# Seven early head pairs instead of six, query maxima as rows of one small product, key-value sums turned through DRAM

## The chip, the cores and the metric

The kernel runs on one core of one Trainium2 chip. The metric is the device time of one execution in microseconds (us), the median of three runs. The core's five instruction queues run side by side and meet at semaphores: TensorE (PE, with PEld for its weight loads), VectorE (DVE), ScalarE (ACT), GpSimd (POOL) and SyncE (SP), which here issues every DMA. Each queue runs its instructions in the order in which they were written.

## The reference

Linear attention over 8 batches, 8 heads, 576 tokens and head size 64, followed by a feed-forward block over all 4608 tokens:

```python
def phi(x):
    proj = np.einsum('bhsd,df->bhsf', x, w_phi)            # 64 -> 128 features
    proj = proj - np.max(np.abs(proj), axis=-1, keepdims=True)
    return np.concatenate([np.exp(proj), np.exp(-proj)], axis=-1)
q_p, k_p = phi(q), phi(k)
kv = np.einsum('bhsf,bhsd->bhfd', k_p, v)
z = np.sum(k_p, axis=2)
num = np.einsum('bhsf,bhfd->bhsd', q_p, kv)
den = np.einsum('bhsf,bhf->bhs', q_p, z)[..., None] + 1e-06
attn = num / den
# then, with x = attn as 4608 x 512:
g = np.maximum(x @ w_in, 0.0) ** 2                         # 512 -> 2048
out = g @ w_out                                            # 2048 -> 512
```

So each token's query projection loses its own largest absolute value over the 128 features before the two exponentials.

## The kernel before, in words

**Work units.** Two heads make a pair; there are 32 pairs, four to a batch. Each pair's result (576 tokens x 128 columns, transposed) goes into a ring buffer in SBUF as two float16 parts (`ring`, lines L733 and L736). The feed-forward block takes the tokens in 18 chunks of 256, each chunk in 8 slices of 256 hidden columns. A slice is one `gemm1` (24 matmuls, L912), three elementwise steps on ACT and DVE (L921 to L930, and the subtraction at L266), and one `gemm2` (12 matmuls, L940). A chunk needs all four pairs of its batch: chunks 0 and 1 lie in batch 0 (pairs 0 to 3), chunk 2 needs pairs 4 to 7 too.

**Early pairs.** The first `EARLY` = 6 pairs run in a form of their own (function `early`), while the feed-forward weights are still being prepared and POOL is not yet free for reductions. A pair's steps are: key projection on PE (`k_main` L490, `k_tail` L496) with maxima, subtraction and exponentials; key-value sums on PE (`kv_main` L546, `kv_tail` L551) and the sums over tokens (L578); then three copies that turn the 128 x 384 result around: ACT copies it from PSUM (`kvs`, L585), PE transposes three blocks (L590), ACT copies them back (`kz`, L593). The query is projected twice. First with tokens on the partitions (L605, tail L611), only so that DVE can take each token's maximum (`qm`, L616 and L620); then, per half of 288 tokens, with features on the partitions (L634). The second projection has the maximum of its own column subtracted by further matmuls into the same PSUM bank: the maxima stand as columns of `qm`, spread over 128 columns, times a negated identity `nident` (L643, six matmuls per half). Exponentials (L650, L652), numerators (L660) and denominators (L678) follow. The denominators go out and back through DRAM: `den<-sx` (L686), `rd<-rc` (L699), `rb<-rd` (L706, two DMAs). A product with the numerators (L714) gives the values that are written to the ring.

For the first `BANKS` = 4 pairs the first projections use PSUM banks that the feed-forward block needs later (`po`, `ph`). Later pairs use the single `pp` buffer, which all second projections use too, so there one user must have been read out before the next one may start.

**Late pairs.** Pairs 6 to 31 run in another form (`visit` and `late`): the key sums are turned by a DVE transpose (L797), one DMA to DRAM (`td`, L798) and eight DMAs back (`kz<-td`, L803), and the query maxima are taken by POOL (`partition_all_reduce`, L846).

**Weights.** Each of the 16 weight blocks is loaded raw (L381, L384; 1024 KB each) and passes through four or five steps on ACT (L401, L390, L422, L426, L435), two or three on DVE (L393, L397, L428) and one or two on POOL (L404, L266).

**What sets the order.** Every step is an `Op` with an engine, a written-down duration, a rank and a landing time for DMAs. `Plan.order` is a list scheduler that runs once on the host; it starts what is ready in the order of rank and writes the instructions of all queues in that order. Ranks are `PER_PAIR` = 4.5 per pair; weight blocks start at rank `PREP0` = 18; feed-forward slices at `LEAD` = 36.

```python
o = P.add("PE", 2.0, q_proj, [q_load[p], minus] + most, [("q", p), pq, ("qm", p)], R(x), mode=(ROWS, WHOLE))
kz = P.add("ACT", act_us(384), lambda: A.activation(
    out=kz_[p], in_=pv_["t", p][:, 0:384], func=AF.Copy), [o], [("pv", ("t", p)), ("kz", p)], R(3.1))
ld = P.add("SP", 2.7, load, [] if of_in else [raw_read[f]], [], rank - 3.0 + 0.3 * n, land=2.0)
```

## Time and profile before

| | |
|---|---|
| median of 3 runs (lowest, highest) | 1113.24 us (1112.3, 1113.45) |
| the profiled execution's own time | 1108.32 us |
| its span, first to last instruction | 1106.5 us |
| mean granted TensorE clock | 0.984 |
| busy: PE, DVE, ACT, POOL | 97%, 67%, 57%, 17% of the span |
| first `gemm1` | at 112.37 us |

The profile is one execution. Its own time is 1.8 us more than its span, and 4.9 us under the median of the runs. In the tables of stretches the columns after the stretch are its length and then, for PE, PEld, DVE, ACT and POOL, the busy time with the number of instructions, and at the end the granted clock (1.00 is full), the DMA share and GB/s. In a timeline a row is start, duration, engine, line, operation, output and inputs, count, and in square brackets the idle time before it with what ended that.

### The profile page before, as it was taken

The numbers are of one execution on the slowest core, as the hardware profiler recorded it, in microseconds if no ns is written. First come the engines' busy times: TensorE is split into PE (matmuls) and PEld (weight loads), VectorE is DVE, ScalarE is ACT, GpSimd is POOL, SyncE is SP. The second block draws the span as 40 slices with busy tenths as digits, with TensorE's granted clock in tenths as the row PEclk, the third lists the DMA queues.
The fourth block names the chain that finished last, engine by engine and source line by source line (L and its number), as shares of the span: only waits on it lengthen the run. The fifth ranks groups of instructions, "written<-read, shape, count | busy, mean of one in ns | idle before, by whom it ended". The sixth has DMA issues, their size and how long they took to land.

```text
span 1106.5 us, 19979 instructions
## 1 busy us (share of the span) xinstructions
PE 1071.9 (97%) x7882; PEld 831.4 (75%) x7882; DVE 739.1 (67%) x1538; ACT 633.5 (57%) x1125; POOL 183.9 (17%) x86
## 2 busy tenths in 40 slices
PE   7868999989999999999999999999999999999998
PEld 5645777767777777777777787777777777888886
DVE  6385988887787888787877687667786875121111
ACT  6787766555656666566665566655554655333332
POOL 1165533111102112111201111110111111000000
PEclk9987999999999999999999999999999999999999
DMA  9733312122122222121221111212111110000000
GB/s 336 266 104 121 104 56 73 55 74 55 55 73 55 73 55 74 55 74 54 74 53 62 36 52 55 74 55 73 43 48 30 36 32 30 11 20 20 1 20 20
DMA packets 68289, 73.50 MB, mean 66 GB/s; under 512 B 36836, under 2 KB 41828, under 8 KB 68196
## 3 DMA queue, kind: packets, MB, share of 16 engines
q1 hardware_dynamic: 68196, 72.23, 21.4%
q8 instruction: 62, 1.02, 0.4%
q14 instruction: 31, 0.25, 0.1%
HBM read 59.18 MB, written 12.99 MB: 65 GB/s over the span
## 4 chain that ended last, share of the span: by engine, by line
PE 74%; DVE 9%; ACT 3%; DMA 3%; issue 2%; POOL 1%; SPq 0%; DVEq 0%; POOLq 0%; ACTq 0%
PE po L940 31%; PE ph L912 29%; PE pv L546 3%; PE pp L833 2%; PE pn L764 2%; PE pp L490 2%; PE pv L764 2%; DMA rb<-rd 1%; PE pv L551 1%; DVE gl L266 1%; DVE pt L860 1%; PE pn L496 1%; DVE qe L266 1%; POOL mx L846 1%; DVE yt L864 1%
## 5 line engine op out<-in xcount | busy, mean ns | idle before, releaser
L912 PE MATMUL ph<-ring,win 128*128 128x256 f16 x3456 | 401.1, 273 | 0.3 <-DVE ring L736 0.3
L912 PEld LDWEIGHTS <-win 128*128 128x128 f16 x3456 | 328.4, 98 | 69.7 <-issue 32.8
L940 PE MATMUL po<-wout,gh 128*128 128x512 f32 x1152 | 371.2, 403 | 0.0
L940 PEld LDWEIGHTS po<-wout,gh 128*128 128x128 f32 x1152 | 207.1, 189 | 47.7 <-issue 5.3
L940 PE MATMUL po<-wout,gl 128*128 128x512 f32 x576 | 227.1, 394 | 3.5 <-DVE gl L266 3.5
L921 ACT ACTIVATE r<-ph,cw 128x512 f32<-128x512 f32 x144 | 98.6, 685 | 223.8 <-PE ph L912 223.4
L846 POOL PARTITION_ALL_REDUCE mx<-pt x52 | 113.8, 2188 | 638.9 <-ACT pt L840 602.6
L266 DVE TENSOR_TENSOR gl<-ph,gh 128x512 fp32r<-128x512 f32 x144 | 98.5, 684 | 158.4 <-ACT ph L930 156.4
L940 PEld LDWEIGHTS po<-wout,gl 128*128 128x128 f32 x576 | 108.6, 189 | 29.1 <-DVE gl L266 4.0
L923 ACT ACTIVATE gh<-r 128x512 fp32r<-128x512 f32 x144 | 90.9, 632 | 4.6
L930 ACT ACTIVATE ph<-r 128x512 f32<-128x512 f32 x128 | 74.7, 583 | 0.0
L786 ACT ACTIVATE n<-pn 128x320 f32<-128x320 f32 x26 | 11.4, 437 | 93.6 <-PE pn L764 93.6
L546 PE MATMUL pv<-e,v 128*64 128x256 f32 x512 | 62.8, 389 | 1.4 <-ACT kz L593 1.4
L266 DVE TENSOR_TENSOR qe<-pt,mx 128x576 f32<-128x576 f32 x52 | 39.3, 755 | 23.0 <-POOL mx L846 22.7
L860 DVE SCALAR_TENSOR_TENSOR pt<-qe,zc,pt 128x576 f32<-128x576 f32 x52 | 42.2, 812 | 12.8 <-ACT pt L858 11.9
L546 PEld LDWEIGHTS pv<-e,v 128*64 128x64 f32 x512 | 36.6, 141 | 18.0 <-issue 2.5
L851 ACT ACTIVATE qe<-qe 128x576 f32<-128x576 f32 x52 | 35.2, 676 | 24.8 <-DVE qe L266 24.6
L512 ACT ACTIVATE e<-e 128x512 f32<-128x512 f32 x64 | 39.7, 621 | 16.1 <-DVE e L509 16.1
L797 DVE STREAM_TRANSPOSE kvs<-pv 128x256 f32<-128x256 f32 x26 | 11.6, 445 | 54.1 <-PE pv L764 48.4
L858 ACT ACTIVATE pt<-qe,zc 128x576 f32<-128x576 f32 x52 | 39.9, 772 | 3.8
L537 DVE TENSOR_TENSOR es<-es,et 64x256 f32<-64x256 f32 x52 | 35.4, 681 | 9.8 <-ACT et L524 8.3
L864 DVE STREAM_TRANSPOSE yt<-pt 128x576 f32<-128x576 f32 x52 | 40.4, 778 | 1.5
(196 smaller groups left out, 1306.4 us busy)
## 6 DMA issues: line engine op xcount, KB each, us to landing
v<-in_vp_dram SPq DMA_DIRECT2D x32, 320.0 KB
k<-in_kp_dram SPq DMA_DIRECT2D x32, 288.0 KB
q<-in_qp_dram SPq DMA_DIRECT2D x32, 288.0 KB
rb<-rd SPq DMA_DIRECT2D x64, 144.0 KB
out_dram<-o SPq DMA_DIRECT2D x36, 256.0 KB
td<-kvs SPq DMA_DIRECT2D x26, 128.0 KB
kz<-td SPq DMA_DIRECT2D x208, 16.0 KB
raw0i<-in_w_in_dram SPq DMA_DIRECT2D x1, 1024.0 KB
```

The costliest lines, as they stand in the source:

```text
L266: eng.tensor_tensor(out=out_, in0=a, in1=b_, op=ALU.subtract)
L546: PE.matmul(out=to[64 * h:64 * h + 64, 0:256], lhsT=v_[p][:, t, h, :], rhs=e_[2 * p + h][:, t].rearrange("p s f -> p (s f)"), start=t == 0 ...
L764: PE.matmul(out=to[64 * h:64 * h + 64, :], lhsT=kz_[n][:, 128 * s_ + 64 * h:128 * s_ + 64 * h + 64], rhs=qe_[2 * n + h].rearrange("p (s x) ...
L846: o = P.add("POOL", par_us(S), lambda n=n, h=h: G.partition_all_reduce(mx_[n], pt_[p][:, h, :], channels=128, reduce_op=bass_isa.ReduceOp. ...
L858: o = P.add("ACT", act_us(S, 1), lambda h=h, qe=qe, y=y: A.activation(out=y(), in_=qe(0), func=AF.Copy, scale=zc_[p][:, 2 * h:2 * h + 1]), ...
L860: o = P.add("DVE", dve_us(S), lambda h=h, qe=qe, y=y: V.scalar_tensor_tensor(out=y(), in0=qe(1), scalar=zc_[p][:, 2 * h + 1:2 * h + 2], in ...
L864: o = P.add("DVE", dve_us(S), lambda n=n, y=y: V.transpose(yt_["y", n - 2 * EARLY], y()), [o], [("pt", p), ("yt", ("y", n - 2 * EARLY))], ...
L912: PE.matmul(out=ph[:, j, :], lhsT=win[w][:, t, 128 * ff:128 * ff + 128], rhs=ring[half][x][:, t, c0:c0 + T], start=k == 0, stop=k == 3 * K ...
L921: o = P.add("ACT", act_us(512, 1), lambda: A.activation(out=r_[n], in_=ph_[bank], func=AF.Relu, scale=cw[:, f, 0:1]), [g1], [("ph", bank), ...
L923: sq = P.add("ACT", act_us(512), lambda: A.activation(out=gh_[n], in_=r_[n], func=AF.Square), [o], [("r", n), ("gh", n)], Q)
L930: o = P.add("ACT", act_us(512), lambda: A.activation(out=ph_[bank], in_=r_[n], func=AF.Square), [sq], [("ph", bank), ("r", n)], Q)
L940: PE.matmul(out=po_[po[i][1]], lhsT=g[n][:, j, 128 * i:128 * i + 128], rhs=wout[f][w][:, j, :], start=(ff == 0 and s == 0), stop=(ff == 2 ...
```

## The change

- `EARLY` goes from 6 to 7 and `BANKS` from 4 to 5. One pair more takes the early form, and five pairs instead of four have their first projections in the feed-forward block's PSUM banks and their last product on POOL.
- The query maxima become rows. DVE transposes the 128 x 32 tile `qm` into `qt`; one DMA writes it to DRAM (`tq`); four DMAs read it back into row 0 and row 64 of a tile `pt` that is otherwise zero. Per half and head one matmul of 64 rows and 288 columns with a stationary operand of -1 subtracts them (`minus`, `row_of`), where six matmuls stood.
- The early pairs' key-value sums are turned as in the late form, with three blocks: a DVE transpose of 384 columns, one DMA to DRAM and twelve back, in place of two ACT copies and three PE transposes.
- The raw weight loads are written down as waiting for each other in the plan, with a landing time of 4.5 instead of 2.0. This concerns the plan's order alone; no semaphore is added.
- `Plan.improve` builds 400 orders with randomly moved ranks, for steps of rank below 70, and keeps the one that the plan holds to be shortest. Some written-down durations, `COLD` and `PREP0` change too.

```diff
-EARLY = 6
-BANKS = 4
+EARLY = 7
+BANKS = 5
+TRIALS, SEED, MOVED = 400, 1, 70.0
+QLAND = 2.4
...
+    def improve(self, trials, seed):
+
+        rnd = random.Random(seed)
+        best, plan = None, None
+        some = [op for op in self.ops if -50.0 < op.rank < MOVED]
+        for n in range(trials):
+            moved = rnd.sample(some, len(some) // 20) if n else []
+            old = [(op, op.rank) for op in moved]
+            for op in moved:
+                op.rank += rnd.gauss(0.0, 1.5)
+            order = self.order()
+            length = max(op.end for op in self.ops)
+            if best is None or length <= best:
+                best, plan = length, order
+            else:
+                for op, rank in old:
+                    op.rank = rank
+        return plan
...
-        ld = P.add("SP", 2.7, load, [] if of_in else [raw_read[f]], [], rank - 3.0 + 0.3 * n, land=2.0)
+        ld = raw_load[0] = P.add("SP", 0.3, load, raw_load + ([] if of_in else [raw_read[f]]), [], rank - 3.0 + 0.3 * n,
+                                 land=4.5)
...
-        o = P.add("ACT", act_us(384), lambda: A.activation(out=kvs_[p], in_=pv_["s", p][:, 0:384], func=AF.Copy),
-                  [o], [("pv", ("s", p)), ("kvs", p)], R(2.6))
-
-        def flip():
-            for g in range(3):
-                PE.transpose(pv_["t", p][:, 128 * g:128 * g + 128], kvs_[p][:, 128 * g:128 * g + 128], ident)
-
-        o = P.add("PE", 0.35, flip, [o, pool_start], [("kvs", p), ("pv", ("t", p))], R(3.0))
-        kz = P.add("ACT", act_us(384), lambda: A.activation(
-            out=kz_[p], in_=pv_["t", p][:, 0:384], func=AF.Copy), [o], [("pv", ("t", p)), ("kz", p)], R(3.1))
+        turn(p, 3, o, ("pv", ("s", p)), lambda: pv_["s", p][:, 0:384], R(2.6))
+        kz = kz_of[p]
...
+        o = P.add("DVE", 0.15, lambda: V.transpose(qt_[p], qm[p % 2]), most, [("qm", p), ("qt", p)], R(1.2))
+        row_of = lambda h, cs: pt_[0][64 * h:64 * h + 64, p % 2, cs]
+
+        o = P.add("SP", 0.1, lambda: SP.dma_start(tq_[p], qt_[p]), [o], [("qt", p), ("tq", p)], R(1.2), land=QLAND)
+
+        def spread_rows():
+            for h in range(2):
+                row = pt_[0][64 * h:64 * h + 1, p % 2, :]
+                SP.dma_start(row[:, 0:512].rearrange("o (t a x) -> o t a x", t=4, a=4),
+                             tq_[p].rearrange("(a c) x -> c a x", a=4)[4 * h:4 * h + 4].unsqueeze(0))
+                SP.dma_start(row[:, 512:S].rearrange("o (a x) -> o a x", a=2),
+                             tq_[p].rearrange("(h a c) x -> h c a x", h=2, a=2)[h, 8:9])
+
+        most = P.add("SP", 0.4, spread_rows, [o], [("tq", p), ("row", p), ("pt", 0)], R(1.2), land=QLAND)
...
                 for h in range(2):
-                    for t in range(5):
-                        lo, hi = max(cs.start, 128 * t), min(cs.stop, 128 * t + 128)
-                        if lo < hi:
-
-                            i, r, d = (4 * h + t, 0, lo - 128 * t) if t < 4 else (8, 64 * h, 64 * h)
-                            rows = slice(r, 128 if t < 4 else r + 64)
-                            PE.matmul(out=pp_["q", n][:, h, lo - cs.start:hi - cs.start],
-                                      lhsT=qm_[p][rows, i:i + 1].to_broadcast([rows.stop - r, 128]),
-                                      rhs=nident[rows, d:d + hi - lo], start=False, stop=hi == cs.stop)
+                    PE.matmul(out=pp_["q", n][:, h, 0:SH], lhsT=minus[64 * h:64 * h + 64, :].to_broadcast([64, 128]), rhs=row_of(h, cs),
+                              start=False, stop=True)
...
-    def turn(p, v, key, src, rank):
+    def turn(p, blocks, v, key, src, rank):
...
+        n = 128 * blocks
+        o = P.add("DVE", dve_us(n), lambda: V.transpose(kvs_[p][:, 0:n], src()), [v], [key, ("kvs", p)], rank)
+        o = P.add("SP", 0.1, lambda: SP.dma_start(td_[p][:, 0:n], kvs_[p][:, 0:n]), [o], [("kvs", p), ("td", p)], rank,
+                  land=2.2)
...
-        kz_of[p] = P.add("SP", 0.8, place, [o], [("td", p), ("kz", p)], rank, land=2.2)
+        kz_of[p] = P.add("SP", 0.4 * blocks, place, [o], [("td", p), ("kz", p)], rank, land=2.2)
...
-        for op in P.order():
+        for op in P.improve(TRIALS, SEED):
             op.fn()
...
-PREP0, PREP1 = 18.0, 1.0
+PREP0, PREP1 = 16.0, 1.0
```

In the three places below the names are those of the tiles, and a number behind a name only tells one use of a tile from another. The first place is TensorE at the second projections of pair 4. Before:

```order
L634 MATMUL pp_976<-q_667,wraw 128x288 x2
L643 MATMUL pp_976<-nident,qm_900 128x128 x2
L643 MATMUL pp_976<-nident,qm_900 128x32
L643 MATMUL pp_976<-nident,qm_900 128x128 x2
L643 MATMUL pp_976<-nident,qm_900 128x32
L590 MATMUL pv_994<-ident,kvs_965 128x128 x3
L353 MATMUL pn_998<-ident,wm_108 128x128
L634 MATMUL pp_1017<-q_667,wraw 128x288 x2
```

The same steps in the changed kernel, where L670 is the projection, L673 the product with the row, L689 a numerator, L524 and L631 the tails of key and query, and L518 pair 5's keys:

```order
L670 MATMUL pp_1001<-q_715,wraw 128x288 x2
L673 MATMUL pp_1001<-pt_95,minus 128x288 x2
L524 MATMUL pn_1008<-wraw,k_583 64x128 x2
L670 MATMUL pp_1019<-q_715,wraw 128x288 x2
L673 MATMUL pp_1019<-pt_95,minus 128x288 x2
L689 MATMUL pv_1035<-qe_899,kz_808 64x288 x4
L631 MATMUL pn_1061<-wraw,q_897 64x128 x2
L518 MATMUL pp_1071<-wraw,k_583 128x128 x8
```

The six narrow matmuls of each half and the three transposes are gone, and two matmuls of the projection's own shape stand in their place. Other pairs' steps move in between.

The second place is TensorE after pair 3's second projections, where the two pairs behind it begin. Before, pair 4's keys (L490) and queries (L605) follow each other in the single `pp` buffer, ahead of pair 3's numerators (L660):

```order
L353 MATMUL pn_823<-ident,wm_107 128x128
L496 MATMUL pn_838<-wraw,k_576 64x128 x2
L490 MATMUL pp_843<-wraw,k_472 128x128 x8
L605 MATMUL pp_883<-wraw,q_667 128x128 x8
L660 MATMUL pn_895<-qe_782,kz_767 64x288 x4
```

In the changed kernel pair 4's keys and queries stand earlier, in `po` and `ph`, and at this place only pair 5's queries (L625) use `pp`, ahead of pair 3's denominators (L707):

```order
L670 MATMUL pp_881<-q_531,wraw 128x288 x2
L673 MATMUL pp_881<-pt_95,minus 128x288 x2
L689 MATMUL pv_892<-qe_717,kz_643 64x288 x4
L524 MATMUL pn_903<-wraw,k_460 64x128 x2
L625 MATMUL pp_915<-wraw,q_897 128x128 x8
L707 MATMUL pn_929<-qe_853,kz_808 32x288
```

Two users of `pp` in a row have become one.

The third place is SP's queue around pair 3's denominators (`den`, `rd`, `rb`), which the first `gemm1` needs. Before:

```order
L483 DMA q_825<-in_qp_dram 128x576
L482 DMA k_855<-in_kp_dram 128x576
L384 DMA raw3o<-in_w_out_dram 128x2x1024
L447 DMA v_963<-in_vp_dram 128x640
L686 DMA den_986<-sx_974 128x1x9
L699 DMA rd_1012<-rc_1003 128x9
L706 DMA rb_1029<-rd_1012 64x2x288 x2
```

In the changed kernel, where `td` and `kz` are pair 4's key-value sums and `tq` pair 5's query maxima:

```order
L715 DMA den_959<-sx_954 128x1x9
L475 DMA v_1006<-in_vp_dram 128x640
L728 DMA rd_1016<-rc_999 128x9
L828 DMA td_1026<-kvs_1014 128x384
L411 DMA raw3o<-in_w_out_dram 128x2x1024
L511 DMA q_1041<-in_qp_dram 128x576
L735 DMA rb_1045<-rd_1016 64x2x288 x2
L834 DMA kz_1048<-td_1026 32x4x32 x12
L648 DMA tq_1082<-qt_1080 128x32
```

Up to the `rb` of pair 3 the queue held 52 DMA issues before and holds 128 now; 48 of these are the four earlier `kz` groups and 25 the query rows of five pairs.

More of the change, by code (lines that the diff above doesn't have):

```diff
@@ L1 @@
 import heapq
+import random
 from contextlib import ExitStack
@@ L184, in order @@
                 continue
-            op.start, op.end = t, t + op.us * (COLD if e == "PE" and t < 100.0 else 1.0)
+            op.start, op.end = t, t + op.us * (COLD if e == "PE" and t < 125.0 else 1.0)
             if op.lock is not None:
@@ L272, in tile_kernel @@
     ones = cp.tile([128, 32], F32, name="ones")
-    nident = cp.tile([128, 128], F32, name="nident")
+    minus = cp.tile([128, 1], F32, name="minus")
+    qm = [cp.tile([128, 32], F32, name=f"qm{i}") for i in range(2)]
     mask = cp.tile([128, 2, 32], F32, name="mask")
@@ L331, in tile_kernel @@
     V.memset(ones, 1.0)
+    V.memset(minus, -1.0)
+    for x in qm:
+        V.memset(x, 0.0)
+    V.memset(pt_[0], 0.0)
     V.memset(dq, 0.0)
@@ L339, in tile_kernel @@
     pool_start = P.add("POOL", 10.8, lambda: None, [], [], -100.0)
-    minus = P.add("DVE", 0.25, lambda: V.tensor_scalar(out=nident, in0=ident, scalar1=-1.0, scalar2=None, op0=ALU.mult),
-                  [pool_start], [], 0.8)
     power_n = [0]
@@ L914, in gemm1 @@
                         k += 1
-        g1 = P.add("PE", 2.60, gemm1, after, [("ph", bank)], m)
+        g1 = P.add("PE", 2.58, gemm1, after, [("ph", bank)], m)
         if f:
```

61 lines of the change are left out of this document (31 added, 30 removed).

## Prediction

> **What bounds the kernel now.** I read the table of stretches first, then TensorE's timeline in the two stretches that lose time, then the queues that its waits lead to.
>
> ```profile
> 0.00:14.00 14.00, 7.80 (x65) 6.95 (x67) 5.69 (x16) 7.53 (x13) 0.68 (x6) 1.00 0.87 300
> 14.00:70.00 56.00, 52.12 (x575) 35.69 (x572) 31.65 (x62) 45.41 (x82) 14.81 (x7) 0.97 0.74 258
> 70.00:112.40 42.40, 28.39 (x226) 18.83 (x227) 30.30 (x43) 33.22 (x52) 25.40 (x10) 0.72 0.31 100
> 112.40:237.20 124.80, 124.29 (x940) 95.35 (x939) 108.52 (x208) 75.64 (x128) 37.99 (x15) 1.00 0.24 73
> 237.20:252.00 14.80, 10.96 (x64) 8.40 (x64) 11.79 (x26) 9.32 (x17) 4.69 (x2) 0.80 0.18 59
> 252.00:1106.50 854.50, 848.33 (x6025) 666.22 (x6023) 551.10 (x1187) 462.38 (x837) 100.33 (x46) 1.00 0.17 47
> ```
>
> TensorE is the bound over nearly the whole span. From the first `gemm1` at 112.4 to 237.2 it is busy for 124.3 of 124.8 us, and after 252 for 848.3 of 854.5. The losses are in two places. The opening, up to 112.4, has 24.1 us without a matmul, and in its last stretch the granted clock is 0.72, which costs 28.39 x 0.28 = 7.9 us more: 32 us in all. The stretch 237.2 to 252 has 14.8 - 10.96 = 3.8 us idle and, at clock 0.80, 2.2 us of slow work: 6.0 us.
>
> So the time is the start of the first `gemm1`, plus TensorE's work behind it, plus what is lost behind it. I take the three in turn.
>
> **The opening: what goes.** TensorE's timeline, second projections of two halves and a first projection, at full clock:
>
> ```profile
> 48.33 0.76 PE L634 MATMUL pp<-q,wraw 64*128 64x288 f32 x4
> 49.01 1.52 PE L643 MATMUL pp<-nident,qm 128*128 128x128 f32 x12
> 50.37 0.52 PE L590 MATMUL pv<-ident,kvs 128*128 128x128 f32 x3
> ...
> 56.00 2.07 PE L643 MATMUL pp<-nident,qm 128*128 128x96 f32 x12
> ...
> 58.42 1.16 PE L605 MATMUL ph<-wraw,q 64*128 64x128 f32 x16
> ```
>
> The six narrow matmuls (L643) hold TensorE from 49.01 to 50.37 in one half and for 2.0 in the other (2.07 less the 0.08 by which such rows overlap, as 48.33 + 0.76 and 49.01 show): 3.37 us for each pair. Five pairs go through this ahead of the first `gemm1`: 16.9 us. The product that replaces them has the shape of the projection L634 (64 rows, two heads, 288 columns), which holds TensorE from 48.33 to 49.01: 0.68 us for a half. No row shows a matmul whose stationary operand is one repeated column at 64 rows; L643 repeats one too, at 128 rows, so I take 0.68, and bound it by nothing and by 1.36. The changed order has eleven such halves ahead of the first `gemm1`: 7.5 us. For the transposes the groups of TensorE's work over the whole span:
>
> ```profile
> L643 PE MATMUL pp<-nident,qm 128*128 128x128 f32 (+1 forms) x144 | 23.6, 305 | 0.0
> L590 PE MATMUL pv<-ident,kvs 128*128 128x128 f32 x18 | 3.2, 285 | 0.2 <-ACT n L666 0.2
> L660 PE MATMUL pn<-qe,kz 128*64 128x288 f32 x48 | 8.1, 464 | 1.5 <-ACT sx L684 1.4
> L660 PE MATMUL pv<-qe,kz 128*64 128x288 f32 x48 | 7.0, 414 | 0.0
> L678 PE MATMUL pn<-qe,kz 128*32 128x288 f32 x96 | 7.6, 439 | 0.0
> L578 PE MATMUL pv<-e,ones 128*32 128x128 f32 x192 | 6.5, 276 | 0.0
> L764 PE MATMUL pn<-qe,kz 128*64 128x320 f32 x208 | 32.5, 433 | 0.0
> L764 PE MATMUL pv<-qe,kz 128*64 128x256 f32 x208 | 26.9, 379 | 0.0
> L833 PE MATMUL pp<-q,wraw 64*128 64x512 f32 x104 | 29.4, 640 | 0.8 <-DVE e L509 0.8
> ```
>
> L590 is 3.2 / 6 = 0.53 us for each pair, five times: 2.7. The changed order also puts pair 5's first projection (1.16, row L605) and one more half (0.68) ahead: 1.8. TensorE's work before the first `gemm1` changes by -16.9 - 2.7 + 7.5 + 1.8 = -10.3 us.
>
> **The opening: waits that go.** TensorE's and DVE's timelines:
>
> ```profile
> 74.32 1.22 PE L490 MATMUL pp<-wraw,k 64*128 64x128 f32 x16 [0.76 <-ACT qe L652]
> 82.87 2.08 PE L605 MATMUL pp<-wraw,q 64*128 64x128 f32 x16 [7.33 <-issue]
> ...
> 99.89 1.33 PE L634 MATMUL pp<-q,wraw 64*128 64x288 f32 x4 [3.29 <-ACT qe L652]
> 101.15 3.60 PE L643 MATMUL pp<-nident,qm 128*128 128x96 f32 x12
> ...
> 112.37 2.79 PE L912 MATMUL ph<-ring,win 128*128 128x256 f16 x24
> ```
>
> ```profile
> 76.72 1.83 DVE L428 SCALAR_TENSOR_TENSOR win<-u,cw,win 128x1024 f16<-128x1024 f32 x1
> ...
> 79.08 2.29 DVE L736 SCALAR_TENSOR_TENSOR ring<-rb,cb,ring 128x576 f16<-128x576 f32 x1
> ...
> 82.09 0.67 DVE L509 TENSOR_TENSOR e<-pp,km 128x512 f32<-128x512 f32 x1
> ```
>
> The 7.33 us ahead of 82.87 are put down to "issue", but the order shows the cause: pair 4's queries want `pp`, which pair 4's keys hold until DVE has subtracted their maxima, at 82.09 + 0.67; DVE had a weight step of 1.83 us and a ring step of 2.29 us ahead of it. With five bank sets pair 4 is out of `pp`. What is late next at that place is pair 5's queries, which want `pp` after ACT's exponentials. The matmuls after the gap are slow (2.08 us for L605, against 1.16; 3.60 for L643 against 2.07). The two waits, 7.33 and 3.29, and the 7.9 us of slow clock are 18.5 us that may go.
>
> **The opening: waits that come.** The query rows and the key-value sums now go through DRAM, and SP issues it all in order. A late pair's `td` and `kz`, a denominator's DMA with DVE behind it, and one landing under the weight loads:
>
> ```profile
> 203.72 0.35 SPq L798 DMA_DIRECT2D td<-kvs  x1
> ...
> 205.47 4.68 SPq L803 DMA_DIRECT2D kz<-td  x8
> ```
>
> ```profile
> 35.92 0.34 SPq L699 DMA_DIRECT2D rd<-rc  x1
> ...
> 40.59 1.33 SPq L706 DMA_DIRECT2D rb<-rd  x2
> ...
> 95.50 0.59 SPq L686 DMA_DIRECT2D den<-sx  x1
> ...
> 99.36 1.62 SPq L706 DMA_DIRECT2D rb<-rd  x2
> ```
>
> ```profile
> 97.50 0.17 DVE L695 TENSOR_SCALAR den<-den 128x9 f32<-128x9 f32 x1
> ```
>
> From issuing `td` to issuing `kz` are 1.75 us; eight issues take 4.68, so twelve take 7.0; the landing is 97.50 - 96.09 = 1.4. The turn through DRAM is 10.2 us from DVE's transpose to the numerators. The rows of the maxima are 1.75, four issues (2.3) and 1.4: 5.5 us. Between a pair's last key-value matmul and the first step that wants `kz`, the changed order leaves 6.4 us of matmuls for pair 0 (by the prices above and the timeline), 5.9 for pair 4 and over 10 for the three between. So 3.8 + 4.3 = 8 us show. The row DMAs and the query loads stand on SP behind a `kz` group of 7.0 us at three pairs; following the five queues by hand I find TensorE about 2.5 us late at each: 7.5 us. In all about 16 us come, against 18.5 that go. I take the two as equal. The bounds are a gain of 18.5 (all covered) and a loss as in the SP rival below.
>
> The Trainium skill ("DMA: Bandwidth & Descriptors", section "Anatomy of one DMA — SWDGE (gpsimd) path") gives a DMA a fixed cost of about 2.0 us; by that each of the two trips, with two landings, is some 1.2 us longer than by the rows, and the sum, if half of it shows, about 6 us later. The rows here, at 1.4 us, decide, outside the stretch of weight loads.
>
> What SP itself pays: 25 issues for rows and 48 for `kz` more ahead of the `rb` of pair 3, 128 against 52. ACT loses two copies for each pair, DVE gains a transpose. SP's 52 issues, at 0.34 to 0.585 us, filled under a third of the 112 us before, and DVE and ACT are busy for 62 and 79 of the 98.4 us from 14 to 112.4. The product of pair 4 moves from DVE to POOL, which is busy for 40 of those 98.4 us. With the raw loads spread out, ACT has eight weight steps fewer ahead of pair 3's ring write; they follow behind it, under the feed-forward matmuls.
>
> So the first `gemm1` moves from 112.4 by -10.3, to 102.
>
> **Behind the first `gemm1`: work.** Moved behind it are one more pair's sums over tokens, numerators and denominators: 6.5 / 6 + (8.1 + 7.0) / 6 + 7.6 / 6 = 4.9 us; one late pair's numerators and queries go: (32.5 + 26.9 + 29.4) / 26 = 3.4. One pair's L643 (23.6 / 6 = 3.9) and transposes (0.5) go, and one projection half and three new products come (4 x 0.68 = 2.7). Sum -0.2: I take 0. The feed-forward part is untouched.
>
> **Behind the first `gemm1`: losses.** The 6.0 us at 237 are chunk 2's. Its values come from pair 7:
>
> ```profile
> 207.06 1.13 PE L833 MATMUL pp<-q,wraw 64*128 64x512 f32 x4
> ...
> 236.14 0.76 DVE L714 TENSOR_TENSOR rb<-n,rb 128x576 f32<-128x576 f32 x1 [1.90 <-DMA rb<-rd]
> ```
>
> ```profile
> 247.06 0.80 PE L940 MATMUL po<-wout,gl 128*128 128x512 f32 x1 [3.55 <-DVE gl L266]
> ...
> 270.12 2.79 PE L912 MATMUL ph<-ring,win 128*128 128x256 f16 x24
> ...
> 275.52 2.79 PE L912 MATMUL ph<-ring,win 128*128 128x256 f16 x24
> ```
>
> Pair 7's projection is at 207.06 and its last product waits for `rb` until 236.14, 29 us later; `gemm2` then waits 3.55 us for `gl`, with nothing else queued. In the changed order six slices lie between pair 7's projection and chunk 2's first `gemm1`, at 5.4 us each (270.12 to 275.52), and a visit: over 32 us, and two `gemm2` of chunk 1 and a visit stand between chunk 2's `gemm1` and its `gemm2`. That takes the 6.0 away. Against it I set 3 us of new waits: pair 5's numerators have some 8 us of matmuls to cover the 10.2 (2 us), and pair 7's come 13 us behind its projection, where 18.5 were (1 us). If weights came late instead there would be more, but TensorE has about 70 us of work in that part for the last eight weight blocks.
>
> **Sum.** -10.3 + 0 - 6.0 + 3 = -13. The span becomes 1093 us. The profiled execution's own time was 1.8 us over its span and 4.9 under the median; with the same distances the median is 1113.2 - 13 = **1100 us**.
>
> **The rivals.** *SP becomes the bound (slower).* 128 issues at 0.34 to 0.585 us are 44 to 75 us; I take 65, and SP itself waits for some 13 landings (`td` to `kz`, `tq` to rows, `rd` to `rb`) by the `rb` of pair 3; the first `gemm1` came 13 us behind it (99.36 to 112.37). At 1.4 us a landing this makes 65 + 18 + 13 = 96, and with 8 us of waits for engines 104. Under the weight loads a landing took 4.3 us (36.26 to 40.59). At a mean of 2.9 it is 124, and the kernel takes 1113.2 + 11.6 - 6 + 3 = 1122 us. It decides from a mean of about 2 us. For it: DMA shares of 0.87 and 0.74 up to 70 us. Against it: the raw loads now stand further apart in SP's queue. Chance 0.14.
>
> *The opening is bound by latency, not by TensorE (about no change).* The 10.3 us turn into idle time, as ACT's weight steps and their landings set the pace: 1113.2 - 6 + 3 = 1110 us. For it: only 28 of 42 us busy from 70 on. The same comes out if the search's order gains nothing on the chip. Chance 0.13.
>
> *New waits leave the clock low.* Six new waits, each followed by slow rows as behind 99.89 (1.33 + 3.60 against 0.76 + 2.07, 2.1 us), cost 12.6 where I kept 7.9: 1105 us. The Trainium skill ("TensorE: Matmul & The Clock Gate", section "Part 1: The HAM clock gate") halves the clock after about 3.4 us idle; the 7.33 and 3.29 us gaps here fit that. Chance 0.10.
>
> *The DRAM trips are covered (faster still).* Half of the 18.5 us stay away: 1091 us. For it: less weight traffic in the first 40 us. Chance 0.13.
>
> **How the numbers follow.** My forecast has 0.50, with a range of its own from 1094 to 1106. 1088 to 1114 reaches to all but the SP rival and the far end of the better one. A measurement tells about 0.2%, 2.2 us, from no change. Faster: 0.50 + 0.13 + 0.10 and half of the 1110 case, 0.79; same: the other half, 0.07; slower 0.14.
>
> **What would show it.** Right: the first `gemm1` at 98 to 106; L643's time replaced by about 10 us of L673; no gap of 7 us at pair 4's queries; no wait for `gl` near chunk 2; TensorE over 99% busy from there. Wrong: the first `gemm1` later than 110, waits of the numerators or of L673 for DMAs of over 5 us each, SP without a pause, or idle time between the first `gemm1` and chunk 2 over 6 us.

## The result, and the profile after

The changed kernel takes 1149.72 us (median of 4 runs, 1148.46 to 1150.49), the kernel before 1112.77 on the same chip (4 runs, 1108.9 to 1113.45): ratio 1.0338, 95% interval 1.0313 to 1.0364. It is 37 us slower, where 13 us less were forecast. In the profiled execution the span is 1148.0 us against 1106.5, the mean granted clock 0.960 against 0.984.

The table of stretches of the changed kernel (length of the stretch, then busy time and number of instructions of PE, PEld, DVE, ACT and POOL, then the granted clock, the DMA share and GB/s):

```profile
14.00:70.00 56.00, 36.27 (x382) 23.62 (x380) 22.89 (x48) 29.05 (x54) 9.26 (x5) 0.77 0.54 162
70.00:112.40 42.40, 22.19 (x194) 14.06 (x194) 18.71 (x40) 21.66 (x36) 13.88 (x7) 0.70 0.40 113
112.40:150.00 37.60, 27.11 (x238) 16.02 (x232) 21.62 (x37) 24.14 (x38) 13.43 (x6) 0.79 0.53 164
150.00:200.00 50.00, 41.90 (x370) 30.90 (x364) 34.78 (x50) 31.60 (x47) 24.61 (x10) 0.90 0.41 129
200.00:237.00 37.00, 30.74 (x196) 21.37 (x197) 23.00 (x58) 16.72 (x32) 7.36 (x3) 0.86 0.19 49
237.00:252.00 15.00, 15.00 (x110) 12.32 (x109) 9.41 (x15) 10.94 (x19) 4.30 (x2) 1.00 0.23 67
252.00:1200.00 948.00, 890.41 (x6322) 700.79 (x6320) 583.77 (x1261) 485.01 (x875) 104.78 (x48) 1.00 0.16 45
```

From 252 on nothing is lost that was not lost before: 896.0 - 890.4 = 5.6 us idle, 6.2 before. Chunk 2's stall is gone (15.00 of 15.00 busy). Everything is lost ahead of 237, and not only up to the first `gemm1`: the three stretches from there to 237 have gaps too. The same stretch as one row, of the kernel before and of the changed one:

```profile
0.00:237.00 237.00, 212.39 (x1796) 156.80 (x1796) 175.96 (x327) 161.60 (x272) 78.88 (x38) 0.94 0.41 135
```

```profile
0.00:237.00 237.00, 165.40 (x1424) 112.02 (x1425) 127.84 (x249) 130.05 (x215) 69.22 (x35) 0.81 0.45 137
```

TensorE idles 71.6 us there in place of 24.6, and the mean granted clock is 0.81 in place of 0.94. (That clock is a mean over idle time too, so it can't be turned into a loss by taking it times the busy time.) Busy time over the whole span, before and changed:

```profile
PE 1071.9 (97%) x7882; PEld 831.4 (75%) x7882; DVE 739.1 (67%) x1538; ACT 633.5 (57%) x1125; POOL 183.9 (17%) x86
```

```profile
PE 1070.8 (93%) x7852; PEld 825.1 (72%) x7852; DVE 721.0 (63%) x1524; ACT 626.0 (55%) x1109; POOL 178.3 (16%) x85
```

TensorE is busy for 1.1 us less than before, where some 10 were forecast. The span is 41.5 us longer, so the loss is idle time. Up to 237 DVE and ACT are less busy than before in the same time, so neither has become the bound. TensorE's waits up to 240 us (total, number of times, longest) name what has:

```profile
PE pp L625 <- DMA q<-in_qp_dram: 14.6, 1, 14.6
PE ph L625 <- DMA q<-in_qp_dram: 12.1, 2, 8.6
PE pn L689 <- DMA kz<-td: 11.6, 2, 7.8
PE pp L673 <- DMA pt<-tq: 10.0, 4, 6.4
PE pn L707 <- DMA kz<-td: 9.5, 2, 7.2
```

These are 57.8 us of waits for DMAs; only 31.1 of them are for the new trips (`kz`, `pt`). The largest, 26.7, are for plain loads of queries that need nothing but to be issued. TensorE's timeline shows the long waits and the first `gemm1` (L943):

```profile
110.09 2.08 PE L625 MATMUL pp<-wraw,q 64*128 64x128 f32 x16 [14.63 <-DMA q<-in_qp_dram]
...
141.92 2.79 PE L943 MATMUL ph<-ring,win 128*128 128x256 f16 x24
...
171.43 2.19 PE L689 MATMUL pn<-qe,kz 128*64 128x288 f32 x8 [7.80 <-DMA kz<-td]
...
177.79 1.19 PE L689 MATMUL pv<-qe,kz 128*64 128x288 f32 x8
...
206.11 1.33 PE L673 MATMUL pp<-pt,minus 64*128 64x288 f32 x2 [6.41 <-DMA pt<-tq]
```

The first `gemm1` stands at 141.92, 29.6 us later than before. Why was the load for 110.09 so late? SyncE's timeline between the loads of two pairs' queries (the second column is how long the issues take):

```profile
78.68 0.38 SPq L511 DMA_DIRECT2D q<-in_qp_dram  x1
...
83.70 0.38 SPq L828 DMA_DIRECT2D td<-kvs  x1
84.14 0.60 SPq L715 DMA_DIRECT2D den<-sx  x1
87.13 6.57 SPq L834 DMA_DIRECT2D kz<-td  x12
93.79 0.40 SPq L411 DMA_DIRECT2D raw2o<-in_w_out_dram  x1
94.28 0.42 SPq L728 DMA_DIRECT2D rd<-rc  x1
94.80 0.38 SPq L648 DMA_DIRECT2D tq<-qt  x1
99.50 1.30 SPq L735 DMA_DIRECT2D rb<-rd  x2
100.89 0.65 SPq L653 DMA_DIRECT2D pt<-tq  x1
...
103.50 0.41 SPq L408 DMA_DIRECT2D raw4i<-in_w_in_dram  x1
103.96 0.51 SPq L511 DMA_DIRECT2D q<-in_qp_dram  x1
```

This is to be read as one queue. `kz` cannot go out before `td` has landed: one short issue stands between them, and SyncE waits 2.4 us (84.74 to 87.13). Twelve issues take 6.57. `rb` cannot go out before `rd` has landed: one issue stands between them, and SyncE waits 4.3 us (95.18 to 99.50). Four row issues follow, a weight load, and then the load of pair 5's queries, which TensorE waits for from 95.5 on. It goes out only at 103.96, half a microsecond behind a load of 1024 KB, and TensorE starts 6.1 us after that. So of the 14.6 us of this wait 8.5 lie ahead of the issue. From one load to the next are 25.3 us. SyncE's waits up to 150 us have three such heads:

```profile
SPq L735 <- DMA rd<-rc: 13.3, 4, 5.2
SPq L834 <- DMA td<-kvs: 9.6, 4, 3.7
SPq L653 <- DMA tq<-qt: 7.0, 4, 2.3
```

The Trainium skill ("DMA: Bandwidth & Descriptors", section "Rules for kernel authors") advises to issue a DMA early and to wait on its semaphore late. Here the order does the opposite, at 29.9 us in twelve waits.

### The profile page after: what moved, and what is told of

Same layout as the page of the kernel before. It is cut to its first block, busy times and chain, and to the rows that moved or that the text cites. A ratio compares the mean times of both kernels' runs of the same rounds, so it can differ in the third digit from the quotient of the medians.

```text
span 1148.0 us, 20042 instructions
## 1 busy us (share of the span) xinstructions
PE 1070.8 (93%) x7852; PEld 825.1 (72%) x7852; DVE 721.0 (63%) x1524; ACT 626.0 (55%) x1109; POOL 178.3 (16%) x85
## 4 chain that ended last, share of the span: by engine, by line
PE 87%; DMA 7%; SPq 3%; ACT 1%; DVE 1%; issue 1%; POOL 0%; DVEq 0%
PE po L971 35%; PE ph L943 32%; PE pv L574 4%; PE pp L518 2%; PE pn L793 2%; PE pp L864 2%; SPq L834 2%; PE pv L793 2%; DMA td<-kvs 2%; PE pv L579 1%; DMA rd<-rc 1%; DMA pt<-tq 1%; PE pn L689 1%; PE pn L524 1%; DMA q<-in_qp_dram 1%; DMA k<-in_kp_dram 1%
## 5 line engine op out<-in xcount | busy, mean ns | idle before, releaser
L943 PE MATMUL ph<-ring,win 128*128 128x256 f16 x3456 | 399.2, 273 | 0.0
L943 PEld LDWEIGHTS <-win 128*128 128x128 f16 x3456 | 328.3, 98 | 67.9 <-issue 30.3
L877 POOL PARTITION_ALL_REDUCE mx<-pt x50 | 109.1, 2181 | 639.1 <-ACT pt L871 571.1
L971 PEld LDWEIGHTS po<-wout,gl 128*128 128x128 f32 x576 | 108.9, 189 | 25.3
L891 DVE SCALAR_TENSOR_TENSOR pt<-qe,zc,pt 128x576 f32<-128x576 f32 x50 | 40.7, 814 | 18.5 <-ACT pt L889 17.7
L540 ACT ACTIVATE e<-e 128x512 f32<-128x512 f32 x64 | 39.7, 622 | 22.0 <-DVE e L537 21.8
L827 DVE STREAM_TRANSPOSE kvs<-pv 128x256 f32<-128x256 f32 (+1 forms) x32 | 15.2, 474 | 54.3 <-PE pv L793 42.7
L542 ACT ACTIVATE e<-e 128x512 f32<-128x512 f32 x64 | 40.2, 628 | 1.4
L556 DVE TENSOR_TENSOR ez<-e 128x512 f32<-128x512 f32 x50 | 36.8, 736 | 4.7 <-ACT e L542 3.7
```

What stands on the lines that cost most here:

```text
L540: o = P.add("ACT", act_us(512), lambda n=n: A.activation(out=e_[n][:, :, 1, :], in_=e_[n][:, :, 0, :], func=AF.Exp, scale=-1.0), [o], [("e ...
L542: exps[p].append(P.add("ACT", act_us(512), lambda n=n: A.activation(out=e_[n][:, :, 0, :], in_=e_[n][:, :, 0, :], func=AF.Exp), [o], [("e" ...
L877: o = P.add("POOL", par_us(S), lambda n=n, h=h: G.partition_all_reduce(mx_[n], pt_[p - EARLY + 1][:, h, :], channels=128, reduce_op=bass_i ...
L891: o = P.add("DVE", dve_us(S), lambda h=h, qe=qe, y=y: V.scalar_tensor_tensor(out=y(), in0=qe(1), scalar=zc_[p][:, 2 * h + 1:2 * h + 2], in ...
L943: PE.matmul(out=ph[:, j, :], lhsT=win[w][:, t, 128 * ff:128 * ff + 128], rhs=ring[half][x][:, t, c0:c0 + T], start=k == 0, stop=k == 3 * K ...
L971: PE.matmul(out=po_[po[i][1]], lhsT=g[n][:, j, 128 * i:128 * i + 128], rhs=wout[f][w][:, j, :], start=(ff == 0 and s == 0), stop=(ff == 2 ...
```

## The experiments

Theory Q: SyncE's one queue has too much to issue and to wait for, whatever the order. Theory P: the work would fit, but the planner's order is bad, since it prices SyncE's steps too low (`0.4 * blocks`, 1.2 us, for twelve `kz` issues that take 5.5 to 7.3; 0.4 for four row issues that take about 2.6). Theory E: the loss comes with the other edits (seventh early pair, raw loads in turn, searched order). Theory N: the search landed on one unlucky order. Theory L: latency, wherever the issues stand. In each ratio the kernel before, run on the same chip, is 1.

| kernel | us | ratio (95%) |
|---|---|---|
| e1: turn on the chip | 1103.86 | 0.9938 (0.9913 to 0.9963) |
| e2: columns of maxima | 1118.85 | 1.0079 (1.0048 to 1.0109) |
| e3: true prices | 1108.98 | 0.9978 (0.9960 to 0.9996) |
| e4: neither trip | 1099.17 | 0.9897 (0.9869 to 0.9926) |
| e5: no search | 1140.68 | 1.0297 (1.0260 to 1.0334) |
| e6: seed 2 | 1134.88 | 1.0242 (1.0207 to 1.0278) |
| e7: true prices, no search | 1115.14 | 1.0055 (1.0028 to 1.0083) |
| e8: neither trip, true prices | 1108.26 | 1.0006 (0.9977 to 1.0034) |
| e9: `kz` issued by GpSimd | 1131.22 | 1.0194 (1.0152 to 1.0235) |
| e9: `kz` issued by ScalarE | 1148.57 | 1.0345 (1.0296 to 1.0393) |
| e10: true price of `kz` alone | 1120.77 | 1.0103 (1.0072 to 1.0133) |
| e11: all true prices but `kz` | 1126.83 | 1.0153 (1.0112 to 1.0194) |
| e12, e13, e16: true prices, seeds 2, 3, 4 | 1114.56, 1105.69, 1108.54 | 1.0036, 0.9955, 0.9982 |
| e14, e15, e17: neither trip, true prices, seeds 2, 3, 4 | 1102.10, 1100.36, 1102.61 | 0.9936, 0.9922, 0.9923 |

**Which part of the change.** e1 puts the turn on the chip back, e2 the columns of maxima, e4 both.

```diff
# e1
-        turn(p, 3, o, ("pv", ("s", p)), lambda: pv_["s", p][:, 0:384], R(2.6))
-        kz = kz_of[p]
+        o = P.add("ACT", act_us(384), lambda: A.activation(out=kvs_[p], in_=pv_["s", p][:, 0:384], func=AF.Copy),
...
+        o = P.add("PE", 0.35, flip, [o, pool_start], [("kvs", p), ("pv", ("t", p))], R(3.0))
+        kz = P.add("ACT", act_us(384), lambda: A.activation(
# e2: no tq, no spread_rows; in q_proj again
+                                      lhsT=qm_[p][rows, i:i + 1].to_broadcast([rows.stop - r, 128]),
+                                      rhs=nident[rows, d:d + hi - lo], start=False, stop=hi == cs.stop)
```

> The changed kernel with the key-value sums of the seven early pairs turned on the chip again (ScalarE copy, three TensorE flips, ScalarE copy) in place of the DVE transpose and thirteen small DMAs through DRAM; the rows of query maxima, the seven pairs, the raw loads in turn and the searched order stay. Theory Q (SyncE's one queue carries too much: 5.5 to 7.3 us of kz issues a pair and the waits for two landings around them): most of the loss goes, 1105 to 1120 us, the first gemm1 before 122 us, and the issue of pair 5's queries at least 10 us earlier. Theory P (the planner's order is bad because it prices twelve issues at 1.2 us): the same, since the mispriced step is gone. Theory E (the loss comes with the seventh early pair, the raw loads and the searched order, not with the DMAs): 1140 us or more.

> The changed kernel with the query maxima subtracted again by the eight to ten column products of each half, without the tq and row DMAs (five issues a pair, about 3.2 us, and two landings); the turn through DRAM stays. Theory Q: a part of the loss goes, since 3.2 of some 15 us of issues a pair go, while TensorE gets back some 17 us of products of which the waits hide the most: 1125 to 1145 us. Theory P: like the changed kernel, 1140 to 1150, since the mispriced turn stays. Theory E: 1145 or more.

> The changed kernel without both: the turn on the chip and the column products as before; left of the change are the seventh early pair, the raw loads in turn, the new durations and the searched order. Theory Q and theory P: SyncE's queue is as light as in the kernel before, 1105 to 1118 us. Theory E: 1140 or more.

Theory E falls: without both trips the rest of the change is a gain of 1.0%, more than any theory gave it. With the turn on the chip (e1) 4.0% comes back, a little more than was expected. With the columns (e2) 2.6% comes back, and that missed both theories: e2 lies 6 us under theory Q's range and 21 us under theory P's, which took the turn for the only wrong price that matters. Together that is 6.6%, where taking out both trips brings back 4.4%. This speaks against a plain price per issue, which would add up.

**The same work, another order.** e3 changes numbers of the plan, and not one instruction:

```diff
-        kz_of[p] = P.add("SP", 0.4 * blocks, place, [o], [("td", p), ("kz", p)], rank, land=2.2)
+        kz_of[p] = P.add("SP", 2.2 * blocks, place, [o], [("td", p), ("kz", p)], rank, land=2.2)
-        most = P.add("SP", 0.4, spread_rows, [o], [("tq", p), ("row", p), ("pt", 0)], R(1.2), land=QLAND)
+        most = P.add("SP", 2.7, spread_rows, [o], [("tq", p), ("row", p), ("pt", 0)], R(1.2), land=QLAND)
# tq 0.1 -> 0.45, td and rd 0.1 -> 0.5, den 0.1 -> 0.7, rb 0.2 -> 1.35
```

> The changed kernel, all its operations kept; only the planner's durations of SyncE's steps are set to what the trace of the changed kernel shows: 6.6 us for twelve kz issues in place of 1.2, 2.7 for the four row DMAs in place of 0.4, 0.45 to 0.7 for tq, td, rd and den in place of 0.1, 1.35 for rb in place of 0.2. Theory P: the order found with true prices avoids the waits at the head of SyncE's queue (10.5 us for rd, 9.6 for td, 7.0 for tq) and issues the queries in time: 1105 to 1125 us. Theory Q: issues and landings are still there, 1135 to 1150. Theory E: 1145.

3.6%, about 40 us, goes with no DMA taken out: theory P, and theory Q fails as a theory of the loss. SyncE's timeline of e3 between two loads of queries:

```profile
70.35 0.38 SPq L728 DMA_DIRECT2D rd<-rc  x1
70.83 0.38 SPq L511 DMA_DIRECT2D q<-in_qp_dram  x1
72.43 0.32 SPq L828 DMA_DIRECT2D td<-kvs  x1
72.80 0.68 SPq L653 DMA_DIRECT2D pt<-tq  x1
...
75.49 1.30 SPq L735 DMA_DIRECT2D rb<-rd  x2
76.89 6.22 SPq L834 DMA_DIRECT2D kz<-td  x12
...
89.21 0.40 SPq L511 DMA_DIRECT2D q<-in_qp_dram  x1
```

The same issues, but `td` and `rd` now land while the row DMAs go out, and here SyncE waits for neither: `rb` follows the rows at once, `kz` follows `rb`. The load of pair 5's queries, at 89.21, now stands ahead of pair 4's rows, where it stood behind them. From load to load are 18.4 us, in place of 25.3; over four pairs it is 81.0 (28.29 to 109.25) in place of 92.7 (30.11 to 122.84), and the first `gemm1` comes at 122.77. TensorE's waits for query loads, rows and `kz`, 57.8 us before, are absent from e3's list of waits. Its busy time over the whole span, for the same 7852 matmuls:

```profile
PE 1060.7 (96%) x7852; PEld 819.3 (74%) x7852; DVE 728.0 (66%) x1524; ACT 624.8 (56%) x1109; POOL 182.0 (16%) x85
```

The span is 41.4 us shorter than the changed kernel's (1106.6 against 1148.0). TensorE is busy for 10.1 us less, since fewer matmuls run at a low clock; the other 31 us are idle time that went.

**Luck or prices.** e5 and e6 keep the wrong prices and change the order otherwise; e7 has true prices without the search.

```diff
# e5, e7 (e7 with the prices of e3)
-TRIALS, SEED, MOVED = 400, 1, 70.0
+TRIALS, SEED, MOVED = 1, 1, 70.0
# e6
+TRIALS, SEED, MOVED = 400, 2, 70.0
```

> The changed kernel with the planner's first order, without the 400 trials; the wrong prices of SyncE's steps stay. Theory P (wrong prices make the order bad): still slow, 1130 to 1165 us, since the first order is made with the same prices. Theory N (the search by luck landed on an order that the chip dislikes, and another order of the same model would do): within 10 us of the kernel with true prices, 1100 to 1120.

> The changed kernel with the search started from seed 2 in place of 1, wrong prices kept. Theory P: slow again, 1135 to 1165 us. Theory N: anything from 1100 to 1160, and below 1120 would show that the 39 us hang on this one order.

> True prices of SyncE's steps and no search. Theory P: the prices do the work, 1105 to 1125 us, within 15 us of the searched order with true prices (1109), and at least 15 us below the first order with wrong prices. Theory N: no better than the first order with wrong prices.

Theory N falls. Three orders made with wrong prices lie at 1.024 to 1.034; five made with true prices (e3, e7, e12, e13, e16) at 0.996 to 1.006. (e6, at 1134.88, lies just under the 1135 that theory P gave as its lower edge.) Judged by wrong prices, 400 trials gained half a per cent from one seed and lost 0.4% from the other.

**Which price.** e10 has the first line of e3's diff alone, e11 all the others.

> The changed kernel with one number of the planner put right: 6.6 us for the twelve kz issues in place of 1.2 (4.4 for eight in place of 0.8). Theory P: the kz group is 5.4 of some 9 us that a pair's SyncE steps are priced too low, so most comes back: 1110 to 1125 us. If it stays above 1135, the price of kz was not the one that mattered.

> All other prices of SyncE's steps put right (rows 2.7, rb 1.35, tq, td, rd and den 0.45 to 0.7), the kz issues still at 1.2. Theory P: 3.5 to 4 of 9 us a pair, so the smaller part comes back: 1120 to 1140 us.

Each half brings back more than half of it: 2.35% (26 us) with the price of `kz`, 1.85% (21 us) with the rest, 3.5% (39 us) with both (the ratio of e3 and three more seeds is 0.9988 on average, against 1.0338). The two overlap. Each is a single order, so the split is rough.

**Is it SyncE's queue?** The changed kernel's own bad order, with the `kz` issues of the early pairs on another queue. On TensorE the order is row for row the changed kernel's.

```diff
-                    SP.dma_start(kz_[p][32 * b:32 * b + 32, 128 * s:128 * s + 128].rearrange("p (a x) -> p a x", a=4),
+                    (G if p < EARLY else SP).dma_start(kz_[p][32 * b:32 * b + 32, 128 * s:128 * s + 128].rearrange("p (a x) -> p a x", a=4),
# ScalarE: A in place of G
```

> The changed kernel in exactly its slow order on TensorE, VectorE and ScalarE; only the twelve kz issues of the early pairs go out from GpSimd's queue in place of SyncE's. Nothing is taken out of the DMA traffic. Theory P with SyncE's queue as the place (the order was bad because 5.5 to 7.3 us of issues, and the waits for td ahead of them, stand in SyncE's queue before the loads of queries and the rows): 20 us or more come back, 1105 to 1130 us, the load of pair 5's queries is issued at least 8 us earlier than 103.96. Rival L (the latency of the trips and the landings behind the 1 MB weight loads bind, on whichever queue the issues stand): 1140 to 1155. What speaks against a gain here is that GpSimd issues slower, or that its own rounds of the weights come behind the wait for td.

> The same with the twelve kz issues on ScalarE's queue. ScalarE is busy about two thirds of the opening, and every one of its exponentials and copies would stand behind the wait for td and 5.5 to 7.3 us of issues: theory P with the queue as the place expects the wait to move with the issues, so SyncE's waits go but ScalarE's take their place: 1125 to 1160 us. Rival L: 1140 to 1155 as before. Below 1125 would show that only SyncE's queue minds the issues.

From GpSimd, 1.4% (16 us) comes back, where 20 us or more had been expected; the time lies between the ranges of the two theories. The load of pair 5's queries goes out 7.9 us earlier, by SyncE's timeline of that run, where at least 8 had been expected:

```profile
96.09 0.34 SPq L511 DMA_DIRECT2D q<-in_qp_dram  x1
```

TensorE's waits for queries go, but those for `kz` grow to 37.4 us, from 21.1. The trip itself is no shorter: from the issue of `td` to the last of the twelve issues 11.3 to 13.1 us pass in the five pairs up to 140, where it was 9.2 to 12.6 with SyncE.

```profile
PE pn L707 <- DMA kz<-td: 19.6, 3, 10.7
PE pn L689 <- DMA kz<-td: 17.8, 3, 10.0
```

From ScalarE nothing comes back. Both theories allowed that, so the time alone decides nothing. ScalarE's timeline, and TensorE's waits in that run, show where the wait has moved to:

```profile
45.76 8.31 ACTq L834 DMA_DIRECT2D kz<-td  x12
54.12 0.63 ACT L542 ACTIVATE e<-e 128x512 f32<-128x512 f32 x1 [11.07 <-DMA kz<-td]
```

```profile
PE pp L670 <- ACT qe L681: 19.5, 3, 10.5
```

An exponential is held up for 11 us behind the `td` landing and the twelve issues, and TensorE waits for exponentials in place of loads. So the place in a queue costs time. Theory L, by which both would have stayed at 1140 or more, falls as the whole account: two fifths of the loss went with nothing changed but the queue. The other three fifths these two runs don't explain; they went only with another order (e3). The Trainium skill ("DMA: Bandwidth & Descriptors", section "Rules for kernel authors") states that spreading DMAs over issuing engines saves only the issuing sequencer's time. The two runs fit this: SyncE's saved time is worth 16 us with one engine and nothing with the other.

**What the trips cost once they are planned.** e8 is e4 with true prices; e12 to e17 are further orders of e3 and e8.

```diff
# e12, e13, e16: e3 with another seed; e14, e15, e17: e8 with another seed
-TRIALS, SEED, MOVED = 400, 1, 70.0
+TRIALS, SEED, MOVED = 400, 2, 70.0      # 3, 4
```

> The kernel without the turn through DRAM and without the rows (1099 us) with the true prices of the SyncE steps that are left in it (td, kz, rd, rb, den). Theory P: there was little to misprice in the early pairs, so 1096 to 1102, no more than 3 us faster; with the same true prices the kernel with both DMA trips took 1109, so what stays between these two is what the trips cost in themselves: 7 to 13 us (theory Q in a smaller size). If this one comes out at 1106 or more, the trips cost nothing once they are planned.

> True prices with both trips through DRAM, search from seed 2 (seed 1 gave 1109, no search 1115). Theory P: 1104 to 1116 again. If it were above 1125, the true prices had only been lucky with their order.

> The same from seed 3: 1104 to 1116 by theory P. Together with the orders of seeds 1 and 2 it gives the scatter of orders made with true prices.

> True prices without the trips (turn on the chip, column products), search from seed 2; seed 1 gave 1108. If the trips cost 8 us or more in themselves, this one comes out near 1099 and the 1108 was an unlucky order; if they cost nothing once planned, 1104 to 1112.

> The same from seed 3. Three orders with the trips against three without, all with true prices: a difference of the means of more than 6 us shows a price of the trips in themselves, less than 3 shows none that stands out of the scatter of orders.

> True prices with both trips, a fourth order (seed 4). The three before took 0.9978, 1.0036 and 0.9955 of the kernel before, mean 0.9990. If the trips cost 6 us in themselves (0.0055), this one lies at 0.999 plus or minus 0.004, above the other of this pair.

> True prices without the trips, a fourth order (seed 4). The three before took 1.0006, 0.9936 and 0.9922, mean 0.9955. With a price of the trips: 0.993 to 0.997; without one, the two groups' means come within 0.002 of each other.

e8 missed its expectation (1108, where 1096 to 1102 stood): orders of the same work, with the same prices, lie up to 8 us apart. Four orders each average 0.9988 with the trips and 0.9947 without (e17, at 0.9923, a little below what was expected). The gap is 0.0041 or 4.6 us; single orders scatter by 0.0034 and 0.0040, which leaves the gap uncertain by 0.0026. It also lies between the 3 and the 6 us that had been set as bounds, so the times do not settle it. The stretches show its two sides. Of both kinds of kernel the row up to 237, first e3 and then e15:

```profile
0.00:237.00 237.00, 196.78 (x1716) 138.41 (x1717) 159.62 (x303) 153.54 (x257) 79.55 (x39) 0.94 0.49 148
```

```profile
0.00:237.00 237.00, 214.47 (x1919) 157.97 (x1921) 176.61 (x321) 164.79 (x280) 81.83 (x39) 0.98 0.42 136
```

TensorE idles 40.2, 45.8, 33.4 and 39.8 us up to 237 with the trips and 23.6, 20.2, 22.5 and 21.5 without: 17.9 us more on average, with no overlap. Its busy time over the whole span is 1062.7 us with them and 1074.6 without: 11.9 less. The trips, well planned, bring 18 us of idle time for 12 us of busy time saved. That makes 6 us in these eight profiled executions, whose spans overlap (1104.5 to 1115.2 with the trips, 1097.4 to 1105.9 without): a small price of the trips is likely, its size is not settled. Nor is the idle time a wait for the trips' own DMAs, as far as it is named: among TensorE's waits up to 240 us `kz` stands in none of the four lists, and the rows in one, with 0.3 us.

## Why the prediction was wrong

**The bound, and where time can be lost: right.** Behind 252 TensorE idles 5.6 us where 6.2 stood, chunk 2's stall of 6 us went, and no wait for `gl` came back there.

**TensorE's work: right.** -10.3 and -0.2 us were forecast; the four orders with the trips and true prices are busy for 1062.7 us on average, 9.2 less than the kernel before, at nearly the same clock (0.91 to 0.94 up to 237, 0.94 before). In the changed kernel the low clock hides this gain. The new product was taken at 0.68 us a half; at full clock it holds TensorE for 0.58, from TensorE's timeline. L673's total stands in the second fence, from the groups of the whole span:

```profile
156.18 0.65 PE L673 MATMUL pp<-pt,minus 64*128 64x288 f32 x4
156.76 2.79 PE L943 MATMUL ph<-ring,win 128*128 128x256 f16 x24
```

```profile
L673 PE MATMUL pp<-pt,minus 64*128 64x288 f32 x56 | 14.3, 502 | 10.0 <-DMA pt<-tq 10.0
```

It is 14.3 us and not "about 10": fourteen halves at the 0.65 of the first row (which overlaps the next by 0.07) would be 9.1, and the rest is low clock. In e3 the same group takes 9.9.

**The prices of one trip: the issues right, the landings too short.** Twelve issues were put at 7.0 us and take 5.5 to 7.3; the rows' four at 2.3 and take about 2.6. But from issuing `td` to issuing `kz`, and from `tq` to the rows, 1.75 us were taken, from one late pair. In the first four pairs of the changed kernel these are 3.4 to 5.6 and 2.5 to 3.0, by SyncE's timeline. The 2.0 us that the prediction quotes from the Trainium skill ("DMA: Bandwidth & Descriptors", section "Anatomy of one DMA — SWDGE (gpsimd) path") are a figure for DMAs issued by GpSimd, and SyncE issues these.

**"In all about 16 us come, against 18.5 that go ... I take the two as equal": the failed step.** It fails twice. The larger failure is the first number. The 16 us were 8 for `kz` and 7.5 for rows and query loads, ahead of the first `gemm1`. In the changed kernel TensorE waits 43.4 us for them there: 13.3 for `kz`, 3.4 for the rows and 26.7 for query loads. Behind it come 14.4 more for `kz` and rows, where 3 were set. The prediction counted each trip once, by the matmuls that lie beside it on TensorE ("following the five queues by hand I find TensorE about 2.5 us late at each"), and no term held what SyncE's order does to the loads behind it. That order came from a planner that prices twelve issues at 1.2 us, and this line stood in the diff, next to a row of 4.68 us for eight. So waits for landings stood at the head of SyncE's queue, and loads that depend on nothing came behind them. With true prices alone 39 us come back, and the three kinds of wait are gone from e3's list. That the first `gemm1` came later than 110, and that numerators (7.80) and L673 (6.41) waited over 5 us for DMAs, were among the prediction's own signs of being wrong.

The smaller failure is the second number. In the orders without trips, which have the fifth bank set and the raw loads in turn too, TensorE idles 21.9 us up to 237, where 24.6 stood before: about 3 us of waits go, and not 10.6 (the clock term of 7.9 stands beside them; it too was taken from a clock that is a mean over idle time). The waits that the prediction saw were replaced by others as long. So without trips the gain is 0.5% (0.9947), about chunk 2's 6 us, and with well planned trips there is none (0.9988).

That well planned trips bring 17.9 us of idle time, close to the 16 forecast, is luck: the forecast was of waits for `kz`, rows and query loads, and these orders wait 0.3 us at most for the first two, and 5.2 at most for queries. What their idle time comes from was not taken apart.

**The SP rival (1122 us, 0.14): right in kind, too small.** Its condition, a mean landing of over 2 us, held: SyncE's twelve waits average 2.5 us after what stood between. It set the first `gemm1` to 124; 141.92 came. It called SyncE "the bound", and that falls with e3, which has the same issues and 41 us less: SyncE's contents did not bind, their order did.

**The clock rival** (1105 us) is part of the loss: it set 4.7 us for more slow clock, and against e3 the same matmuls take 10.1 us longer. It follows the waits, as in 171.43 above, where a group takes 2.19 us behind a gap of 7.80, and 1.19 at 177.79. The Trainium skill ("TensorE: Matmul & The Clock Gate", section "Part 1: The HAM clock gate") has the clock fall after about 3.4 us idle, and this row agrees. **The latency rival** (1110 us, about no change) names the time that well planned trips come to, 1105.7 to 1114.6 us; whether ACT's weight steps set the pace there, as it had it, was not shown.

**What stays open.** Small DMAs behind a raw load land late, by the rows at the end; how much of the loss would go if no 1024 KB load stood just ahead of them was not tried. Which of the other edits gives the 0.5% beside chunk 2 was not taken apart either. The best version run is e4, the change without both trips, at 0.9897 (0.9869 to 0.9926) of the kernel before; its three siblings with true prices and other seeds lie at 0.992 to 0.994, and one order (e8) at 1.0006.

## What to carry to other kernels

Where a program's order is made from written-down durations, a new step's duration is part of the change: compare it with the trace's row for the same step before you count anything else, since an order made with a wrong price can cost more than the step itself (39 us, against about 5 here that are themselves uncertain). On a queue that runs in order, read what stands between a DMA and the issue that waits for its landing, and what stands behind; loads that depend on nothing belong ahead of such a wait. Where a wait list names plain loads, look up when they were issued: of the 14.6 us here 8.5 were a late queue, and 6.1 the load itself.

## What the runs showed of the hardware

A DMA issue held each of three queues for about as long: twelve `kz` issues took 5.5 to 7.3 us on SyncE in the changed kernel, 6.85 on GpSimd (one uninterrupted group, 26.41 to 33.26) and 5.7 to 8.3 on ScalarE. Not expected was how much later a small DMA lands close behind a raw load. `rd` is a write of 128 x 9 values, and `rb` is issued when it has landed; SyncE's timeline of the changed kernel:

```profile
49.58 0.43 SPq L408 DMA_DIRECT2D raw2i<-in_w_in_dram  x1
50.11 0.45 SPq L728 DMA_DIRECT2D rd<-rc  x1
55.88 1.33 SPq L735 DMA_DIRECT2D rb<-rd  x2
...
75.14 0.38 SPq L728 DMA_DIRECT2D rd<-rc  x1
76.66 1.29 SPq L735 DMA_DIRECT2D rb<-rd  x2
```

From `rd` to `rb` are 5.8 us half a microsecond behind a raw load of 1024 KB, 5.2 in the fence further up, and 4.2 in the kernel before (66.11 to 70.28, 1.1 us behind one). With none issued for 9 us ahead it is 1.5 here (75.14), and 1.4 to 1.5 at four places in the kernel before; at 189.35 in the changed kernel it is 2.7, with a raw load going out 0.4 us behind `rd`. The loads of queries fit: TensorE starts 2.8 us after the issue at 78.68, and 6.1 us after the one at 103.96. This is seen side by side; no run moved the raw loads alone.
